# Another order of the steps in the first part of an attention and two-MoE kernel

## The chip, the cores and the metric

The kernel runs on one core of one Trainium2 chip. The metric is the device time of one execution in microseconds (us), taken as the median of several runs; lower is better. Engines are named as in the profile: PE is TensorE (PEld its weight loads), DVE is VectorE, ACT is ScalarE, POOL is GpSimd, SP is SyncE, which here only issues DMAs. Each engine works through its own queue in order.

## What is computed

Attention inside chunks of 64 positions (8 batches, 8 heads, 576 positions, head size 64), then two feed-forward blocks over the 4608 tokens. Cut to what matters:

```python
scores = 1/sqrt(D) * matmul(q_c, k_c^T)              # per chunk of 64
attn = exp(scores - max(scores)); attn /= sum(attn) + 1e-9
x = matmul(attn, v_c)                                # 4608 tokens x 512
h = maximum(maximum(x @ w1, x @ w2), x @ w3)         # d_ff 768
x = h @ w_out                                        # 512
h = maximum(x @ w_in, 0)                             # d_ff 2048
out = h * h @ w_out2                                 # 4608 x 512
```

## The kernel before

The tokens are cut into 36 attention tiles of 128 and into 9 blocks `b` of 512 tokens, four tiles each. The kernel has three parts in a row: attention with the first feed-forward block (`p` and `y` matmuls, L382), the second block's first product (`z`, L477) and its second (`o`, L528). All products work on numbers that are split into a high and a low half, so a product is three matmuls (high by high, high by low, low by high). Weights come as 64-bit numbers and are converted on the chip.

The change touches the first part's list alone: the string `order` (from L648), which writes out the order of the work for blocks 0 and 1 by hand. The loop at L669 goes through its tokens and issues each step's instructions; `tc.manual_schedule()` (L604) keeps that order in every engine's queue. So a token's place sets the place of its instructions on PE, DVE, ACT, POOL and SP at once, each only among the instructions of the same engine.

The tokens, with the engine that each step uses:

- Tiles 0 to 7 (`tile_steps`, L609). `qk5` and `v5` issue the loads of tile 5 (SP; 0.52 MB for q and k, 0.26 MB for v). `S5` scores (PE); `M5` maximum and difference (DVE, L299 and L302); `X5` exponential (ACT, L305); `N5` sum, plus 1e-9, reciprocal (DVE, L311 to L316); `G5` multiplication (POOL, L319); `T5` turning (PE, L325); `E5` copy of it (ACT, L334); `V5` the product with v, whose tile is named `X` (PE, L353); `H5` and `L5` high half (ACT, L363) and low half (DVE, L368).
- Weight units 0 to 23 (`unit`, L122). `U5` issues the load (SP, L133, 0.52 MB). `A5` takes the number apart (two ACT passes, L95 and L96); `C5` is three DVE instructions (L103, L105, L108); `s5` an addition (POOL, L150); `h5` high half (ACT, L153); `l5` low half (DVE, L156). Units 0, 1, 2 are the slices `w0_0`, `w1_0`, `w2_0` of the three first weights, 3, 4, 5 the slices `_1`, 6 and 7 the slices `wo0` and `wo1` of the output weight, and then four at a time: `w0_f`, `w1_f`, `w2_f`, `wof`.
- Products (`item_steps`, L637). `p` followed by b, f, w multiplies block b by slice f of weight w: 24 matmuls on PE into one of two PSUM buffers of tag "p" (`bufs` in L55). `q000`/`p000` and `q001`/`p001` are two halves of one product each; the `q` half needs tiles 0 and 1 alone. `ep` empties the buffer: for w = 0 a copy `s` on ACT (L410), for w = 1 the maximum `m` on DVE (L413), for w = 2 the maximum `h` on DVE (L417). `hh` and `hl`, followed by b and f, split that `h` (ACT L420, DVE L422). `y3` multiplies block 0's `h` of slice 3 by `wo3` (24 matmuls).
- `@` takes one step of the attention of tiles 8 and up, `~` the softmax work behind it.

Behind the tokens `S1` and `V1` four matmuls on zeros (`heat`, L593) are issued, and eleven ahead of the list. Raw weights go through a ring of four buffers (tag "in"), so a `U` waits for the `C` of an earlier unit.

Of the kernel before, what the change touches and what calls it, by code (L numbers as in the profile page):

```python
# [35 lines left out]
N0 = 2  # L36
# [6 lines left out]
def kernel(ctx: ExitStack, tc, qkv, w123, w_out, w_in2, w_out2, out):  # L43
# [228 lines left out]
    def att_load_v(t):  # L272
        if t >= NT1:
            return
        v = wp.tile([P, 2, 4, D], F32, tag="w", name="v")
        for j in range(2):
            r, o = slice(j * D, j * D + D), (j ^ t % 2) * D
            nc.sync.dma_start(v[o:o + D].rearrange("p c a d -> p (c a d)"), qkv[t, r, 1024:1536])
        v_t[t] = v
# [149 lines left out]
    def g2(b, f):  # L429
        if f == 0:  # L430
            yacc[b] = [ps_tile("acc", f"y{d}") for d in range(KD)]
        hp = h_t.pop((b, f))
        wh, wl = WO[f]
        for d in range(KD):
            a, c = d // 2, slice(d % 2 * P, d % 2 * P + P)
            mm_k(yacc[b][d], (wh[:, a, c], wl[:, a, c]), hp, f, f == 0, f == NF1 - 1)
        if f == NF1 - 1:
            for d in range(KD):
                ys = tmp("ys")
                if d % 2:  # L440
                    nc.vector.tensor_copy(ys, yacc[b][d])
                else:
                    nc.scalar.copy(ys, yacc[b][d])
                nc.sync.dma_start(y_d[b][:, d, :], ys)
            del yacc[b]
# [37 lines left out]
    def take(tag, name):  # L483
        t = tmp(name)
        nc.scalar.copy(t, bank[tag])  # L485
        return t
# [66 lines left out]
    def soften():  # L553

        for g in todo.pop(0) if todo else ():
            run(g)
# [36 lines left out]
    def heat(n):  # L593

        for i in range(n):
            nc.tensor.matmul(warm, lhsT=zero[:, 0:P], rhs=zero, start=True, stop=True)

    def go(*gens):

        for g in gens:  # L600
            next(g, None)
# [35 lines left out]
    def item_steps(b, f, w):  # L637

        for p in proj(W123[f, w], x_t[b], f"p{w}", 2 if (b, f, w) in split_items else 1):
            yield  # L640
        yield from p1_end(b, f, w, p)
# [4 lines left out]


    order = """  # L648
        qk0 qk1 v0 v1 U0 qk2 S0 v2 M0 S1 qk3 X0 v3 M1 N0 X1 U1 N1 A0 G0 U2 G1 T0 C0 S2 E0 qk4 s0
        h0 V0 M2 v4 T1 H0 l0 S3 E1 L0 X2 U3 V1 M3 H1 N2 qk5 X3 A1 L1 G2 v5 N3 q000 A2 C1 G3 qk6 T2  # L650
        S4 E2 v6 C2 s1 h1 V2 M4 qk7 h2 s2 T3 H2 v7 U4 U5 U6 E3 L2 X4 V3 l1 A3 N4 S5 H3 l2 G4 q001
        L3 M5 p000 C3 U7 X5 T4 ep000 S6 E4 N5 s3 h3 V4 M6 G5 S7 H4 l3 X6 T5 L4 p001 E5 N6 A4 M7 V5
        G6 A5 T6 ep001 p002 C4 U8 H5 E6 X7 L5 s4 h4 N7 A6 V6 ep002 G7 A7 p010 l4 C5 U9 H6 hh00 L6
        s5 h5 T7 C6 U10 ep010 p011 E7 A8 l5 s6 hl00 h6 C7 U11 V7 A9 p012 ep011 s7 l6 H7 C8 U12 h7
        A10 y0 L7 s8 h8 ep012 l7 hh01 l8 A11 hl01 p100 C9 U13 C10 U14 s9 h9 A12 p101 l9 s10 ep100
        C11 U15 h10 p102 ep101 h11 s11 l10 A13 C12 U16 p110 ep102 s12 h12 C13 U17 A14 hh10 l12 s13
        h13 p111 l11 ep110 A15 C14 U18 A16 l13 s14 p112 ep111 h14 C15 U19 A17 l14 s15 h15 y1 ep112
        C16 U20 hh11 A18 hl11 s16 h16 p020 C17 U21 A19 l16 s17 l15 h17 p120 C18 U22 ep020 A20 l17
        s18 C19 U23 h18 p021 ep120 A21 l18 s19 C20 h19 p121 ep021 h20 s20 C21 A22 p022 l20 s21 h21
        ep121 A23 l19 l21 C22 p122 ep022 h22 s22 C23 hh02 p030 ep122 h23 s23 hl02 hh12 l22 l23  # L660
        p130 ep030 hl12 hl10 p031 ep130 p131 ep031 y2 ep131 p032 p132 ep032 hh03 hl03 p040 ep132
        hh13 hl13 p140 ep040 p041 ep140 p141 ep041 y3 ep141 p042 p142 ep042 hh04 hl04 p050 ep142
        hh14 hl14 @ p150 ep050 ~ p051 ep150 ~ p151 ep051 @ y4 ep151 p052 @ p152 ep052 hh05 hl05 ~
        y5 ep152 hh15 hl15 ~
    """.split()

    att = steps(8, NT1)
# [1 line left out]
    for token in order:  # L669
        if token == "@":  # L670
            att.pop(0)()
            continue
        if token == "~":
            soften()
            continue
        kind, n = token.rstrip("0123456789"), token.lstrip(ascii_letters)
        if kind == "v":
            att_load_v(int(n))
        elif kind in ("qk", *"SMXNGTEVHL"):
            go(tiles[int(n)])  # L680
        elif kind == "U":
            U[int(n)] = units[int(n)]()
        elif kind in (*"ACshl",):
            U[int(n)][kind]()
        elif kind == "y":
            g2(0, int(n))
        else:
            b, f, w = map(int, (n + "2")[:3])
            if kind == "q" or kind == "p" and (b, f, w) not in items:
                items[b, f, w] = item_steps(b, f, w)  # L690
            go(items[b, f, w])
        if token in ("S1", "V1"):
            heat(4)
        if token == "y3":
            for load in (att_load_v, att_load):
                for t in (8, 9):
                    load(t)
# [48 lines left out]
    for b in range(NB):  # L746
        for g in range(NG):
            bank["at"] = None
            z(b, g, 1, "at", True)
            a, s1 = bank["at"], take("at", "s1")  # L750
# [9 lines left out]
            s5 = take("acc", "s5")  # L760
            next(more, None)
            z(b, g, 6, "at", False)
            s2 = take("at", "s2")
# [84 lines left out]
```

## Time and profile before

| | |
|---|---|
| median of 3 runs | 1397.73 us (1396.68 to 1398.42) |
| the profiled execution | 1396.79 us, span 1395.0 us |
| PE busy | 1369.1 us, 98% |
| DVE busy | 914.6 us, 66% |
| ACT busy | 521.8 us, 37% |
| POOL busy | 195.1 us, 14% |
| granted TensorE clock, mean of the span | 0.998 |

The span is the profiled stretch; the time of the execution holds a little more around it. A busy share is a mean over the three parts, which have different limits, so it has to be read by stretches of time. Matmuls overlap: the next one starts while the last one runs out, so a pause of PE looks a little shorter in busy time than it is.

### The profile page before, as it was taken

The page shows a single profiled execution, that of the slowest core. Times are in us where ns is not written, and L with a number is a line of the kernel's source. Part 1 is how long each engine was busy: PE and PEld are TensorE (multiplying, and loading weights), DVE is VectorE, ACT ScalarE, POOL GpSimd, SP SyncE. Part 2 cuts the span into 40 slices and gives each one's busy share as a digit, 9 for nine tenths or more (in the row PEclk, how much of TensorE's full clock was granted, in tenths as well). Part 3 has the DMA queues.
Part 4 walks back from the last instruction along what each step waited for, and adds up shares of the span by engine and source line. Part 5 has one row for each costly group of instructions (what it writes and reads, how often), then busy time and mean ns, then how long its engine had stood idle before and what let it go on. Part 6 is the DMA issues. An engine that isn't in the chain of part 4 may idle for free.

```text
span 1395.0 us, 32661 instructions
## 1 busy us (share of the span) xinstructions
PE 1369.1 (98%) x13699; PEld 1354.3 (97%) x13699; DVE 914.6 (66%) x1437; ACT 521.8 (37%) x904; POOL 195.1 (14%) x180
## 2 busy tenths in 40 slices
PE   7979999999999999999999999999999999999998
PEld 5879999999999999999999999999999999999998
DVE  7994456566666565723266666667677788877774
ACT  4661234333343343311233333333334444444442
POOL 2440023322423232300000000000000000000000
PEclk9999999999999999999999999999999999999999
DMA  9451244554645554716543333343598443434341
GB/s 270 140 170 43 87 132 148 186 190 140 228 145 181 184 173 131 263 47 228 181 164 124 140 142 143 138 144 136 192 347 300 145 144 123 137 135 152 122 139 43
DMA packets 101235, 222.33 MB, mean 159 GB/s; under 512 B 11232, under 2 KB 20448, under 8 KB 101088
## 3 DMA queue, kind: packets, MB, share of 16 engines
q1 hardware_dynamic: 101088, 220.25, 46.9%
q8 instruction: 107, 1.75, 0.5%
q14 instruction: 40, 0.33, 0.1%
HBM read 134.22 MB, written 85.98 MB: 158 GB/s over the span
## 4 chain that ended last, share of the span: by engine, by line
PE 86%; DVE 1%; issue 0%; POOLq 0%; POOL 0%; ACT 0%; DVEq 0%; ACTq 0%
PE o L528 25%; PE z L477 25%; PE p L382 25%; PE y L382 9%; PE X L353 1%; PE S L292 1%; PE T L325 1%; DVE pl L219 0%; DVE u L500 0%; POOL u L500 0%; POOLq L844 0%; DVE mx L299 0%; DVE sm L311 0%; DVE e L302 0%; DVE h L417 0%
## 5 line engine op out<-in xcount | busy, mean ns | idle before, releaser
L477 PE MATMUL z<-yxh,wih 128*128 128x256 f32 x560 | 154.9, 277 | 0.0
L477 PE MATMUL z<-yxh,wil 128*128 128x256 f32 x560 | 154.7, 276 | 0.0
L477 PE MATMUL z<-yxl,wih 128*128 128x256 f32 x560 | 154.7, 276 | 0.0
L528 PE MATMUL o<-wo2h,gl 128*128 128x256 f32 x504 | 140.7, 279 | 0.0
L528 PE MATMUL o<-wo2h,gh 128*128 128x256 f32 x504 | 140.4, 279 | 0.0
L528 PE MATMUL o<-wo2l,gh 128*128 128x256 f32 x504 | 140.2, 278 | 0.0
L528 PE MATMUL o<-wo2h,gxl 128*128 128x256 f32 x504 | 140.1, 278 | 0.0
L528 PE MATMUL o<-wo2h,gxh 128*128 128x256 f32 x504 | 139.9, 278 | 0.0
L528 PE MATMUL o<-wo2l,gxh 128*128 128x256 f32 x504 | 139.9, 278 | 0.0
L500 DVE TENSOR_TENSOR c<-z,s 128x512 f32<-128x512 f32 x108 | 74.4, 689 | 89.4 <-PE z L477 84.9
L420 ACT CAST hh<-h 128x512 fp32r<-128x512 f32 x54 | 33.6, 621 | 261.7 <-DVE h L417 242.5
L477 PE MATMUL z<-yh,wih 128*128 128x256 f32 x448 | 124.2, 277 | 0.0
L477 PE MATMUL z<-yh,wil 128*128 128x256 f32 x448 | 124.1, 277 | 0.0
L477 PE MATMUL z<-yl,wih 128*128 128x256 f32 x448 | 124.1, 277 | 0.0
L417 DVE TENSOR_TENSOR h<-p,m 128x512 f32<-128x512 f32 x54 | 37.1, 688 | 132.0 <-PE p L382 131.1
L500 POOL TENSOR_TENSOR u<-u,s 128x512 f32<-128x512 f32 x9 | 11.7, 1295 | 761.5 <-DVE u L500 761.5
L485 ACT COPY s<-z 128x512 f32<-128x512 f32 x108 | 63.3, 586 | 133.7 <-PE z L477 132.4
L477 PEld LDWEIGHTS z<-yxh,wih 128*128 128x128 f32 x560 | 105.2, 188 | 0.2 <-DVE c L500 0.2
L477 PEld LDWEIGHTS z<-yxh,wil 128*128 128x128 f32 x560 | 105.1, 188 | 0.0
L477 PEld LDWEIGHTS z<-yxl,wih 128*128 128x128 f32 x560 | 105.1, 188 | 0.0
L528 PEld LDWEIGHTS o<-wo2l,gh 128*128 128x128 f32 x504 | 94.9, 188 | 0.0
L528 PEld LDWEIGHTS o<-wo2h,gl 128*128 128x128 f32 x504 | 94.7, 188 | 0.0
(184 smaller groups left out, 4079.4 us busy)
## 6 DMA issues: line engine op xcount, KB each, us to landing
gd<-g SPq DMA_DIRECT2D x144, 256.0 KB, 2.0
gr<-gd SPq DMA_DIRECT2D x72, 512.0 KB, 4.0
qk<-in_qkv SPq DMA_DIRECT2D x28, 512.0 KB, 3.9
raw<-in_w_out SPq DMA_DIRECT2D x22, 512.0 KB, 3.7
v<-in_qkv SPq DMA_DIRECT2D x72, 128.0 KB, 5.7
raw<-in_w SPq DMA_DIRECT2D x18, 512.0 KB, 3.6
yd<-ys SPq DMA_DIRECT2D x36, 256.0 KB, 2.9
yr<-yd SPq DMA_DIRECT2D x18, 512.0 KB, 5.2
```

What stands on the lines that cost most here:

```text
L292: nc.tensor.matmul(s_t[t][o:o + D, h ^ t % 2, :], lhsT=q[r, h, :], rhs=k[r, h, :], start=True, stop=True,)
L325: nc.tensor.transpose(tp[:, p * P:(p + 1) * P], e[:, 2 * p:2 * p + 2, :].rearrange("p h k -> p (h k)"), ident)
L353: nc.tensor.matmul(xps_t[t][j * D:j * D + D, p, c * D:c * D + D], lhsT=v[o:o + D, c, p, :], rhs=et[o:o + D, p, q:q + D], start=True, stop= ...
L382: nc.tensor.matmul(dst[:, c], lhsT=lhs, rhs=rhs[:, c], start=first and i == 0 and j == 0, stop=last and j == len(pairs) - 1, skip_group_ch ...
L417: nc.vector.tensor_tensor(out=h, in0=p, in1=st[b], op=ALU.max)
L420: nc.scalar.copy(hh, h)
L477: nc.tensor.matmul(dst[:, a * HC:a * HC + HC], lhsT=l[:, a, w], rhs=r[:, k, :], start=first and a + k + j == 0, stop=j == 2, skip_group_ch ...
L485: nc.scalar.copy(t, bank[tag])
L500: (eng or nc.vector).tensor_tensor(out=t, in0=x, in1=y, op=ALU.add)
L528: nc.tensor.matmul(bank[i][:, m * HC:m * HC + HC], lhsT=l[:, a, t], rhs=r[:, a, :], start=g + m + a + j == 0, stop=g == NG - 1 and j == 2, ...
```

## The change

The string is replaced by another one. It holds the same tokens, each once, in another order, and every step issues the same instructions. Besides, the first loads of tiles 8 and 9 are issued behind the token `p041` where they were issued behind `y3`. The diff, cut to the beginning, the middle and the end of the list:

```diff
     order = """
-        qk0 qk1 v0 v1 U0 qk2 S0 v2 M0 S1 qk3 X0 v3 M1 N0 X1 U1 N1 A0 G0 U2 G1 T0 C0 S2 E0 qk4 s0
-        h0 V0 M2 v4 T1 H0 l0 S3 E1 L0 X2 U3 V1 M3 H1 N2 qk5 X3 A1 L1 G2 v5 N3 q000 A2 C1 G3 qk6 T2
...
-        C16 U20 hh11 A18 hl11 s16 h16 p020 C17 U21 A19 l16 s17 l15 h17 p120 C18 U22 ep020 A20 l17
-        s18 C19 U23 h18 p021 ep120 A21 l18 s19 C20 h19 p121 ep021 h20 s20 C21 A22 p022 l20 s21 h21
-        ep121 A23 l19 l21 C22 p122 ep022 h22 s22 C23 hh02 p030 ep122 h23 s23 hl02 hh12 l22 l23
...
-        y5 ep152 hh15 hl15 ~
+        U1 qk0 U2 U0 qk1 qk3 qk2 qk4 qk5 v0 v1 qk7 qk6 v2 v3 A1 C1 S0 s1 U5 v4 U3 M0 v5 A2 h1 C2 A0 l1
+        X0 C0 S1 M1 s0 U4 v7 U6 S3 N0 X1 S2 N1 G0 M3 G1 T0 S4 M2 X3 E0 S5 N3 X2 h0 T1 N2 V0 E1 G3 M4 V1
+        G2 T3 M5 X4 S7 s2 H1 H0 T2 N4 S6 E2 L0 h2 G4 X5 L1 V2 E3 l0 T4 M7 H2 V3 E4 q000 N5 H3 A5 L3 G5
+        V4 L2 C5 q001 H4 A3 T5 M6 s5 U9 v6 p000 C3 X6 A4 p001 N6 U7 ep000 X7 G6 E5 N7 T6 G7 ep001 V5 E6
+        l2 h5 T7 L4 s3 H5 V6 h3 p002 l3 H6 C4 E7 h4 s4 U8 p010 ep002 A6 l4 A7 L5 L6 p011 C7 A8 l5 ep010
+        U11 C6 V7 p012 H7 ep011 s6 U10 h6 L7 h7 s7 A9 p100 l6 ep012 C8 p101 C9 h8 U12 ep100 hh01 s9 A10
...
+        hl05 ~ y5 hh14 hh15 hl15 hl14 hl13 ~
     """.split()
...
-        if token == "y3":
+        if token == "p041":
```

How this moves the queues is shown at two places. The first is the beginning of SP's queue, which sets when data lands; `raw` is a weight unit, `q` and `k` are a tile's. Before:

```order
L265 DMA q_111<-in_qkv 128x512
L265 DMA k_112<-in_qkv 128x512
L265 DMA q_115<-in_qkv 128x512
L265 DMA k_116<-in_qkv 128x512
L278 DMA v_119<-in_qkv 64x512 x2
L278 DMA v_122<-in_qkv 64x512 x2
L133 DMA raw_127<-in_w123 128x1024
L265 DMA q_129<-in_qkv 128x512
```

Now:

```order
L133 DMA raw_113<-in_w123 128x1024
L265 DMA q_115<-in_qkv 128x512
L265 DMA k_116<-in_qkv 128x512
L133 DMA raw_121<-in_w123 128x1024
L133 DMA raw_125<-in_w123 128x1024
L265 DMA q_127<-in_qkv 128x512
L265 DMA k_128<-in_qkv 128x512
L265 DMA q_131<-in_qkv 128x512
```

Unit 1 has gone ahead of tile 0's q and k, units 2 and 0 ahead of tile 1's; the loads of v follow behind six tiles' q and k.

The second is DVE's queue at the steps that empty the PSUM buffers of the products of slice 2, with block 0's `m` and `h` of `p021` and `p022`. Before, from `l21` to the `h` of `p122`:

```order
L156 TENSOR_TENSOR w_5l<-r,w_5h 128x2x256
L103 TENSOR_SCALAR a<-a 128x512
L105 TENSOR_SCALAR a<-a 128x512
L108 SCALAR_TENSOR_TENSOR a<-raw,a 128x512
L417 TENSOR_TENSOR h<-p_1423,m_1412 128x512
L103 TENSOR_SCALAR a<-a 128x512
L105 TENSOR_SCALAR a<-a 128x512
L108 SCALAR_TENSOR_TENSOR a<-raw,a 128x512
L417 TENSOR_TENSOR h<-p_1462,m_1451 128x512
```

Now, from the `m` of `p021` on:

```order
L413 TENSOR_TENSOR m_1267<-p_1202,s_1157 128x512
L103 TENSOR_SCALAR a<-a 128x512
L105 TENSOR_SCALAR a<-a 128x512
L108 SCALAR_TENSOR_TENSOR a<-raw,a 128x512
L417 TENSOR_TENSOR h<-p_1240,m_1267 128x512
L156 TENSOR_TENSOR wo2l<-r,wo2h 128x512
L103 TENSOR_SCALAR a<-a 128x512
```

Before, the `h` of `p022` stands behind `C22`, the last conversion but one; now it stands behind `C15`, with nine conversions still to come.

## Rows read from the trace of the kernel before

**Rows 1.** The page, part 1: busy us (share of the span) and instructions.

```profile
PE 1369.1 (98%) x13699; PEld 1354.3 (97%) x13699; DVE 914.6 (66%) x1437; ACT 521.8 (37%) x904; POOL 195.1 (14%) x180
```

**Rows 2.** Windows: stretch, length, busy us of PE, PEld, DVE, ACT, POOL; clock, DMA.

```profile
0.00:25.00 25.00, 18.25 (x279) 13.28 (x281) 16.32 (x31) 10.65 (x18) 6.16 (x11) 0.93 0.95 266
25.00:50.00 25.00, 21.32 (x363) 20.18 (x359) 24.24 (x44) 17.27 (x32) 10.71 (x9) 1.00 0.63 180
50.00:75.00 25.00, 22.24 (x205) 21.19 (x205) 24.48 (x36) 14.51 (x26) 9.70 (x8) 1.00 0.49 153
75.00:100.00 25.00, 19.50 (x160) 18.69 (x158) 24.48 (x35) 14.95 (x27) 10.50 (x7) 1.00 0.52 167
100.00:125.00 25.00, 23.11 (x194) 22.68 (x195) 15.77 (x24) 6.95 (x12) 5.37 (x4) 1.00 0.35 101
125.00:1395.00 1270.00, 1264.71 (x12512) 1258.25 (x12510) 809.31 (x1272) 457.48 (x793) 152.71 (x142) 1.00 0.46 158
```

**Rows 3.** Waits of PE, 0 to 200 us: total, times, longest.

```profile
PE p L382 <- DVE m L413: 4.4, 3, 2.8
PE T L325 <- POOL e L319: 4.0, 4, 2.8
PE p L382 <- ACT s L410: 3.2, 3, 2.1
```

**Rows 4.** Timeline around p030: start, duration, engine, line, operation, [idle before <- releaser].

```profile
105.63 0.41 DVE L103 TENSOR_SCALAR a<-a 128x512 f32<-128x512 f32 x1
...
107.15 0.68 DVE L417 TENSOR_TENSOR h<-p,m 128x512 f32<-128x512 f32 x1
...
107.40 1.28 POOL L150 TENSOR_TENSOR r<-a,r 128x512 uint32<-128x512 uint32 x1 [2.85 <-DVE a L108]
107.75 1.22 DVE L103 TENSOR_SCALAR a<-a 128x512 f32<-128x512 f32 x1
...
107.89 0.50 PE L382 MATMUL p<-xh,w_3h 128*128 128x256 f32 x2 [0.83 <-DVE h L417]
```

**Rows 5.** Timeline of the first 32 us: loads' waiters and the durations of single steps.

```profile
5.03 1.15 PE L292 MATMUL S<-k,q 64*64 64x64 f32 x32
...
7.43 1.15 PE L292 MATMUL S<-k,q 64*64 64x64 f32 x32 [1.25 <-DMA k<-in_qkv]
...
10.95 0.67 ACT L95 ACTIVATE a<-raw 128x512 f32<-128x512 f32 x1 [0.25 <-DMA raw<-in_w]
...
12.31 0.66 PE L325 MATMUL T<-ident,e 128*128 128x128 f32 x4 [2.77 <-POOL e L319]
...
13.41 1.33 PE L292 MATMUL S<-k,q 64*64 64x64 f32 x32 [0.45 <-DMA k<-in_qkv]
...
14.47 1.98 PE L353 MATMUL X<-et,v 64*64 64x64 f32 x32
...
18.49 1.10 PE L353 MATMUL X<-et,v 64*64 64x64 f32 x32
...
18.71 0.69 DVE L299 TENSOR_REDUCE mx<-S 128x8 f32<-128x512 f32 x1 [0.91 <-PE S L292]
...
20.04 0.68 DVE L311 TENSOR_REDUCE sm<-e 128x8 f32<-128x512 f32 x1
...
21.08 0.64 DVE L368 TENSOR_TENSOR xl<-X,xh 128x512 fp32r<-128x512 f32 x1
...
21.30 1.05 POOL L319 TENSOR_TENSOR e<-e,rs 128x512 f32<-128x512 f32 x1 [5.16 <-DVE rs L316]
...
31.47 0.68 DVE L368 TENSOR_TENSOR xl<-X,xh 128x512 fp32r<-128x512 f32 x1
```

**Rows 6.** The chain that ended last: two of its pieces behind the list.

```profile
612.35 8.28 PE p L382 x72
...
623.35 8.28 PE p L382 x72
```

**Rows 7.** DMA in the first 40 us.

```profile
DMA packets 4741, 10.56 MB, mean 264 GB/s; under 512 B 640, under 2 KB 640, under 8 KB 4736
```

More of the change, by code (lines that the diff above doesn't have):

```diff
@@ L648 @@
     order = """
-        qk0 qk1 v0 v1 U0 qk2 S0 v2 M0 S1 qk3 X0 v3 M1 N0 X1 U1 N1 A0 G0 U2 G1 T0 C0 S2 E0 qk4 s0
-        h0 V0 M2 v4 T1 H0 l0 S3 E1 L0 X2 U3 V1 M3 H1 N2 qk5 X3 A1 L1 G2 v5 N3 q000 A2 C1 G3 qk6 T2
-        S4 E2 v6 C2 s1 h1 V2 M4 qk7 h2 s2 T3 H2 v7 U4 U5 U6 E3 L2 X4 V3 l1 A3 N4 S5 H3 l2 G4 q001
-        L3 M5 p000 C3 U7 X5 T4 ep000 S6 E4 N5 s3 h3 V4 M6 G5 S7 H4 l3 X6 T5 L4 p001 E5 N6 A4 M7 V5
-        G6 A5 T6 ep001 p002 C4 U8 H5 E6 X7 L5 s4 h4 N7 A6 V6 ep002 G7 A7 p010 l4 C5 U9 H6 hh00 L6
@@ L654 @@
[L654 to L657, printed above, removed]
-        C16 U20 hh11 A18 hl11 s16 h16 p020 C17 U21 A19 l16 s17 l15 h17 p120 C18 U22 ep020 A20 l17
-        s18 C19 U23 h18 p021 ep120 A21 l18 s19 C20 h19 p121 ep021 h20 s20 C21 A22 p022 l20 s21 h21
@@ L660 @@
-        ep121 A23 l19 l21 C22 p122 ep022 h22 s22 C23 hh02 p030 ep122 h23 s23 hl02 hh12 l22 l23
-        p130 ep030 hl12 hl10 p031 ep130 p131 ep031 y2 ep131 p032 p132 ep032 hh03 hl03 p040 ep132
-        hh13 hl13 p140 ep040 p041 ep140 p141 ep041 y3 ep141 p042 p142 ep042 hh04 hl04 p050 ep142
-        hh14 hl14 @ p150 ep050 ~ p051 ep150 ~ p151 ep051 @ y4 ep151 p052 @ p152 ep052 hh05 hl05 ~
-        y5 ep152 hh15 hl15 ~
+        U1 qk0 U2 U0 qk1 qk3 qk2 qk4 qk5 v0 v1 qk7 qk6 v2 v3 A1 C1 S0 s1 U5 v4 U3 M0 v5 A2 h1 C2 A0 l1
@@ new lines @@
+        p102 hl01 h9 ep101 s8 hh00 l9 A11 p110 ep102 l7 C10 A12 p111 ep110 l8 U14 C12 p020 s10 ep111 h12
+        C11 p112 hl00 h11 U15 U13 s12 ep020 h10 s11 p120 ep112 l10 A14 A15 C14 p021 ep120 s14 U18 h14
+        A13 l14 p022 hh11 l12 ep021 C15 p030 ep022 s15 U19 U16 hh02 h15 l11 C13 y0 h13 s13 U17 ep030
+        p121 l13 A16 hl02 C16 p031 ep121 h16 s16 A17 p122 ep031 hh10 hl11 A18 A19 y1 C19 l15 p130 ep122
+        C18 C17 h18 p032 ep130 s18 h17 U21 U22 U20 U23 p131 s17 s19 y2 ep131 l18 ep032 l17 p132 l16 A21
@@ L665 @@
+        hh03 C21 p140 ep132 h21 s21 h19 l21 p141 ep140 A20 p142 ep141 p040 ep142 C20 hl10 h20 p041 s20
+        hh13 ep040 l20 A23 hl03 p042 A22 ep041 y3 ep042 l19 C23 p050 @ h23 hh04 hl04 C22 p150 ep050 ~
+        s22 s23 p051 ep150 ~ h22 hh12 l22 hl12 p151 @ l23 ep051 p152 ep151 p052 @ y4 ep052 ep152 hh05
+        hl05 ~ y5 hh14 hh15 hl15 hl14 hl13 ~
     """.split()
```

## The prediction

> **What bounds the kernel now.** I read the page first, then the time cut into windows, then TensorE's waits, then the timeline at the largest waits. TensorE (PE) is busy for 1369.1 of 1395.0 us [rows 1], so all its idle time together is 25.9 us. The windows say where it lies [rows 2]: 6.75, 3.68, 2.76, 5.50 and 1.89 us in the first five stretches of 25 us, 20.6 us in all; in the 1270 us behind them only 5.3 us are left. A list that orders the first part can therefore give back at most some 20 us, 1.5% of the time, and whatever it gives back stays, because the rest is work of PE without gaps: an item that starts earlier ends earlier.
>
> The same windows show the limit of that first part: from 25 to 100 us VectorE (DVE) is busy for 24.2 to 24.5 of each 25 us, PE for 19.5 to 22.2. PE waits for DVE's `m`, for GpSimd's (POOL's) `e` and for ScalarE's (ACT's) copy `s` [rows 3]. `m`, `h` and `s` are what empties a PSUM buffer of tag "p". There are two, so a product can start only when the product two before it has been emptied.
>
> The last such wait shows it whole [rows 4]. DVE goes through the three instructions of `C22` from 105.63, then `h` at 107.15 (this is `ep022`), and p030, the first product on `w_3h`, starts on PE at 107.89, right after `h`. The `h` had stood behind conversions of weights. POOL's instruction from 107.40 then stretches DVE's next one to 1.22 us (the same L103 took 0.41 at 105.63), while `h`, which reads PSUM, kept its 0.68.
>
> **The measure.** I call "delay" of an item the time at which PE starts it, less PE's work that the list puts ahead of it. Prices: a scores step S and an output step V (its tile is `X`) 1.1 us, a turn T 0.55, a little under their durations in [rows 5], since the next step begins while one runs out; a product or a `y` step of 24 matmuls 2.75, as 96 take 11.00 us where nothing is waited for [rows 6]. Ahead of p030 stood 8 tiles (22.0 us) and 20 items (55.0): its delay is 107.89 - 77.0 = 30.9 us. Behind it PE runs on without a gap worth the name [rows 2], so 30.9 us is what the old list costs.
>
> DVE's work by its starts: C 1.52 (105.63 to 107.15), one tensor_tensor 0.60 (107.15 to 107.75) [rows 4]; M 1.33, N 1.04 [rows 5]. A POOL instruction costs DVE something too: from 31.47 [rows 5] to `ep022` at 107.15 DVE has 20 C, 3 M, 3 N and 37 tensor_tensor, 59.9 us, but took 75.7; 22 POOL instructions fall there, 0.72 us each. So old `ep022` ends after 23 C, 8 M, 8 N, 44 tensor_tensor (80.5) and 30 x 0.72, 102.1 us of DVE work; it ended at 107.83, an offset of 5.7. Delay = 102.1 - 77.0 + 5.7 = 30.8, which closes the sum.
>
> **The change, part by part.** No instruction comes or goes; busy sums stay.
>
> *Products.* In the old list whole conversions stand ahead of each release, in the new one they stand behind it where they can. DVE's work ahead of a release, less PE's ahead of the product that needs it, is 16.6 for p110, 16.7 for p020, 23.2 for p022, 25.1 for p030. By the same count the new list has its largest value at p100 (`L7`: 8 C, 8 M, 8 N, 17 tensor_tensor and 15 POOL, 52.2, less 38.5, 13.7), and then 12.4 at p110, 9.5 at p030, 3.4 at p130. The offset comes from the start, walked through next.
>
> *Loads.* Three weight units (0.52 MB each) go ahead of most q and k. S0 started at 5.03 behind 0.52 MB, S1 at 7.43 behind 1.05, S2 at 13.41 behind 2.62, the last two waiting for the transfer [rows 5]: 0.26 MB per us, and the mean of the first 40 us is 264 GB/s [rows 7]. New: unit 1 by 5.0, k0 (1.05 MB) 7.4, k1 (2.62) 13.4, k5 (4.72) 21.4, k6 (6.29) 27.3, v3 (6.82) 29.3, unit 5 31.3. So M1 ends some 7 us later than in the old list; `C1`, `C2`, `C0` fill part of it.
>
> *The clock.* The granted clock of the first 25 us is 0.93 [rows 2]: X at 14.47 took 1.98 us, at 18.49 1.10 [rows 5], half speed (1.2 of 2.4 GHz), after PE had stood idle for 2.77 us before 12.31. The new list leaves PE emptier still between 5 and 15 us, so I put S0, S1 and the four warming matmuls at half speed, which makes M1 0.9 us later (2.0 for 1.1). The Trainium skill (TensorE: Matmul & The Clock Gate, Part 1) says that an idle array falls back to 1.2 GHz, which speaks against this change; the row agrees, and where by that rule PE stayed at 1.2 GHz through its later waits the sum would be that of the second rival.
>
> *DVE's start.* S0 7.4 to 9.4, M0 10.8, C2 12.3, l1 12.9, C0 14.4. S1 13.4 to 15.4, M1 16.8, N0 and N1 18.9, M3 and M2 21.6, N3 and N2 23.7, one POOL hold 24.4, M4 and M5 27.1, N4 28.1, L0, L1, l0 29.9.
>
> *PE's start.* S5 (k5) 21.4 to 22.5, T1, V0, V1 25.3, four warming matmuls 26.3 (1.04 us), T3, S7, T2, S6, V2, T4, V3 32.7; all data has landed by then. q000 starts at 32.7: 16.0 us of work ahead, delay 16.7. That is later than in the old list, but S4 to S7, T2 to T4, V2 and V3 now stand ahead of it.
>
> *To the first full product.* V3's copy H3 on ACT 33.3 (an ACT pass is at most 0.67 [rows 5]), L3, L2 34.5, C5, M6, C3 38.9, N6 39.9; N7 waits for the exponential of tile 7, which stands behind A3, A4 and `ep000` on ACT, until 40.4, and ends 41.9 with a POOL hold; POOL's `e` 43.0 (1.05 [rows 5]); T7, V6, then p002 at 44.8. Work ahead 26.4, delay 18.4. DVE's `l2` ends about 43.6, counted 40.1 (5 C, 8 M, 8 N, 8 tensor_tensor, 12 POOL), an offset of 3.5; at p100 that makes 13.7 + 3.5 = 17.2, below 18.4. From here PE is the later of the two, and each release waits for its product, not for conversions.
>
> *Cover.* PE now hides the conversions. Between p002 and p132 stand 25 items; in the walk some eight releases come within 1.3 us of their need. If none slips, nothing is added; if each slips by one POOL hold, 8 x 0.72 = 5.8. Most margins are nearer 1 than 0, so I take 2.0. Behind the list nothing is late: DVE was busy for 15.8 us in 100:125 [rows 2] and has its last `l` long before p052.
>
> **Sum.** 30.9 - 18.4 - 2.0 = 10.5 us saved. The profiled execution took 1396.79 us (span 1395.0 and 1.8 around it): 1386.3. It lies 0.94 below the median of 1397.73, so I forecast **1387.2 us**. With the hold at 0 and the start 1 to 2 us better or worse its own range is 1384 to 1393.
>
> **Rivals.** *POOL holds DVE in full* (8%). For: L103 at 107.75. Against: the mean of 0.72 over 22. Place: the dense G and s steps before `L7`. At 1.28 us, the whole instruction [rows 4], 15 of them add 8.4 us: delay 13.7 + 8.4 + 3.5 = 25.6, with the 2.0 a gain of 3.3, 1394.4. This is the rule of the Trainium skill (SBUF — State Buffer, section "SBUF: two separate sides"): the pair of ports that both engines share is locked for a whole instruction. The trace agrees on what is held (L103, not `h`), not on the mean price.
>
> *The clock stays low* (6%; slower). If PE keeps 1.2 GHz not to about 17 but up to p002, the 5.1 us from T3 to V3 and the 10.4 from q000 to p002 take twice as long and lie on the path: p002 at about 60, delay 18.4 + 15.5 = 33.9, with the 2.0 5.0 us worse than before, 1402.7. It becomes slower from about 13 us of added PE time on. Against: once PE was busy from 14.47 the old run was back at 1.10 by 18.49.
>
> *The gain is handed on* (7%; no change). ACT's copies `s` stand among the A and h steps that DVE needs, and DVE's releases behind C; if each of the 25 items waits 0.42 us more, 10.5 us are gone, 1397.7. For: waits for `s` of 3.2 us in 3 cases [rows 3]. Against: the walk's margins. If the list on the chip did nothing, the time would be this as well.
>
> *Better* (7%). No slip, and a start 2 us sooner (TensorE at full clock, transfers faster): 30.9 - 17.2 + 1 is 14.7 saved, 1383.0.
>
> **How the numbers follow.** My forecast has 72%. A difference under 0.2% (2.8 us) can't be told from none. Faster: 0.72 + 0.08 + 0.07 = 0.87; same 0.07; slower 0.06. The range 1384.0 to 1394.5 holds the forecast's cases and the first rival; the low clock, the lost gain and most of the better case, some 18%, are left out.
>
> **What would show it.** Right: q000 near 33 and p002 near 45 us; PE's idle time in the first 125 us about 11 instead of 20.6, nearly all of it before 45; DVE below 24 of 25 us between 50 and 100, waiting for PE's `p`; p030 near 85 to 87 instead of 107.9; everything behind 130 us as before, some 10 us earlier. Wrong: PE waits for `m`, `h` or `s` after 50 us of over 4 us in sum (slips or holds), a clock below 0.85 in the first 25 us or below 1.00 in the second (clock), or p002 later than 50.

## The result, and the profile after

The changed kernel took 1383.15 us (median of 4 executions, 1382.38 to 1384.69), the kernel before in the same job 1397.34 us; the ratio is 0.9899, 95% interval 0.9887 to 0.9912. It is faster, by 14.2 us, where 10.5 were forecast. The time lies 0.85 us below the lower end of the range. In a second job (the run `again`, below) the same kernel took 1384.68 us (1383.38 to 1385.24) against 1397.11, 12.4 us less, and that lies inside the range: its own start differs from execution to execution, which the sections below take apart.

The page of the changed kernel, part 1, in the columns of [rows 1]:

```profile
PE 1368.1 (99%) x13699; PEld 1353.8 (98%) x13699; DVE 902.7 (65%) x1437; ACT 520.6 (38%) x904; POOL 194.8 (14%) x180
```

The span fell from 1395.0 to 1382.9 us and PE's work nearly stayed (1369.1 and 1368.1), so what went is PE's idle time. DVE's busy time fell by 11.9 us with the same 1437 instructions; the last section comes back to that.

The windows, in the columns of [rows 2]:

```profile
0.00:25.00 25.00, 16.69 (x281) 11.55 (x282) 18.32 (x36) 10.29 (x17) 8.63 (x13) 0.93 0.95 300
25.00:50.00 25.00, 23.97 (x343) 21.44 (x342) 19.10 (x38) 16.73 (x31) 8.45 (x7) 0.94 0.60 165
50.00:75.00 25.00, 25.00 (x241) 24.80 (x240) 21.89 (x35) 11.77 (x22) 8.51 (x6) 1.00 0.42 126
75.00:100.00 25.00, 25.00 (x220) 25.00 (x219) 16.78 (x30) 14.51 (x26) 6.78 (x5) 1.00 0.33 107
100.00:125.00 25.00, 25.00 (x221) 25.00 (x220) 12.04 (x21) 6.44 (x11) 5.15 (x4) 1.00 0.33 107
```

From 50 to 125 us PE has no gap at all, where [rows 2] show 2.76, 5.50 and 1.89 us idle in three stretches. DVE, which had been busy for 24.5 of 25, is down to 21.9 and 16.8. All that is left of PE's idle time in these 125 us lies in the first two stretches, 8.31 and 1.03 us. The waits of PE over the first 200 us, in the columns of [rows 3], name them:

```profile
PE S L292 <- DMA k<-in_qkv: 4.6, 2, 3.9
PE X L353 <- issue: 2.4, 1, 2.4
PE T L325 <- POOL e L319: 1.5, 2, 1.0
PE warm L596 <- DVE zero L77: 1.2, 1, 1.2
```

No wait for `m`, `s` or `h` is left. At p030, the place of [rows 4], the order of events has turned round; the timeline there, in the same columns:

```profile
84.86 1.29 POOL L150 TENSOR_TENSOR r<-a,r 128x512 uint32<-128x512 uint32 x1 [3.62 <-DVE a L108]
...
84.94 0.39 PE L382 MATMUL p<-xh,w_3h 128*128 128x256 f32 x2
...
85.14 0.69 DVE L417 TENSOR_TENSOR h<-p,m 128x512 f32<-128x512 f32 x1 [0.45 <-PE p L382]
```

PE starts p030 at 84.94 with no wait, and now it is the `h` (of p022) that waits 0.45 us for PE. 84.94 less 66.0 us of work ahead is a delay of 18.9 us, against 30.9: 12.0 less, and the two profiled executions differ by 1396.79 - 1384.69 = 12.1. The measure of the prediction holds.

The start of PE's queue in the changed kernel, in the columns of [rows 5]:

```profile
5.87 1.15 PE L292 MATMUL S<-k,q 64*64 64x64 f32 x32 [0.66 <-DMA k<-in_qkv]
10.94 1.93 PE L292 MATMUL S<-k,q 64*64 64x64 f32 x32 [3.92 <-DMA k<-in_qkv]
12.80 1.84 PE L596 MATMUL warm<-zero 128*128 128x512 bf16 x4
...
19.85 1.15 PE L353 MATMUL X<-et,v 64*64 64x64 f32 x32
23.42 1.15 PE L353 MATMUL X<-et,v 64*64 64x64 f32 x32 [2.42 <-issue]
24.50 1.74 PE L596 MATMUL warm<-zero 128*128 128x512 bf16 x4
26.03 1.06 PE L325 MATMUL T<-ident,e 128*128 128x128 f32 x4
...
41.64 0.66 PE L325 MATMUL T<-ident,e 128*128 128x128 f32 x4 [1.03 <-POOL e L319]
...
44.97 0.50 PE L382 MATMUL p<-xh,w_0h 128*128 128x256 f32 x2
```

S1 started at 10.94, not at 13.4, and ran at half speed (1.93), as did the four warming matmuls behind it. Then V1 (the second `X` row) waited for 2.42 us, and behind that pause the clock fell a second time: the second group of warming matmuls took 1.74 us, T3 1.06. The windows give the granted clock of both stretches:

```profile
11.00:14.50 3.50, 3.50 (x36) 2.11 (x36) 3.09 (x7) 0.69 (x3) 1.26 (x1) 0.51 1.06 390
24.70:28.10 3.40, 3.40 (x28) 2.28 (x28) 2.76 (x6) 0.98 (x2) 1.04 (x1) 0.50 1.05 256
```

p002 came at 44.97, behind 26.4 us of work (delay 18.6), and from there to p030 (delay 18.9) only 0.4 us were added (18.57 to 18.94).

### The profile page after: what moved, and what is told of

Its sections match the earlier page's. It is cut to its first block, busy times and chain, and to the rows that moved or that the text cites. A ratio compares the mean times of both kernels' runs of the same rounds, so it can differ in the third digit from the quotient of the medians.

```text
span 1382.9 us, 32659 instructions
## 1 busy us (share of the span) xinstructions
PE 1368.1 (99%) x13699; PEld 1353.8 (98%) x13699; DVE 902.7 (65%) x1437; ACT 520.6 (38%) x904; POOL 194.8 (14%) x180
## 4 chain that ended last, share of the span: by engine, by line
PE 86%; DVE 1%; issue 0%; POOLq 0%; POOL 0%; ACT 0%; ACTq 0%; DVEq 0%
PE o L528 25%; PE z L477 25%; PE p L382 25%; PE y L382 9%; PE X L353 1%; PE S L292 1%; PE T L325 1%; DVE pl L219 0%; DVE u L500 0%; POOL u L500 0%; POOLq L843 0%; DVE mx L299 0%; DVE sm L311 0%; DVE e L302 0%; DVE h L417 0%
```

## The experiments

Each kernel was timed against the kernel before on the same chip. The delay given is that of p030 in the profiled execution, less 77.0 us of work ahead in the order that the old list has there, 66.0 in the new one.

**Which part of the list brings the gain.** The new list up to p012 with the rest in the old order (`h_newfront`; its diff against the changed kernel is shown), and the reverse (`h_oldfront`).

```diff
         ep010 U11 C6 V7 p012
-        H7 ep011 s6 U10 h6 L7 h7 s7 A9 p100 l6 ep012 C8 p101 C9
+        hh00 U10 s6 hl00 h6 A9 ep011 s7 l6 H7 C8 U12 h7 A10 y0
...
```

> The new list up to p012, then the rest of the tokens in the old list's order. Theory (the gain lies in where DVE's releases of the two PSUM buffers stand among the conversions): the count of DVE's work ahead of the release less PE's ahead of the product is 24.9 us at p030 and 25.0 at p130, with the new front's offset of 3.5 a delay of 28 to 29 us at p030 instead of 18.8, so 9 to 10 us slower than the changed kernel, 1392 to 1394, and PE waits for m, h and s between 60 and 110 us. Rival (the gain lies in the front: loads, tiles, first products): 1383 to 1385, with no such waits.

> The old list up to p012, then the rest in the new list's order. Theory (releases): the largest lag is 14.2 us at p100, with the old front's offset of 5.7 a delay of about 20 us, so 1 to 2 us slower than the changed kernel, 1384 to 1386. Rival (the front): most of the gain is gone, 1393 to 1397.

`h_newfront` took 1395.65 us (ratio 0.9989, 0.9981 to 0.9998), `h_oldfront` 1384.15 us (0.9905, 0.9892 to 0.9919). The windows of 50:75 and 75:100 of `h_newfront`, then two of its waits of PE:

```profile
50.00:75.00 25.00, 22.80 (x211) 21.73 (x209) 23.93 (x36) 15.01 (x28) 10.54 (x8) 1.00 0.49 149
75.00:100.00 25.00, 19.57 (x159) 18.96 (x160) 24.45 (x35) 14.97 (x26) 11.27 (x8) 1.00 0.57 174
```

```profile
PE p L382 <- DVE m L413: 4.4, 3, 2.8
...
PE p L382 <- ACT s L410: 3.0, 3, 1.9
```

and the same windows of `h_oldfront`:

```profile
50.00:75.00 25.00, 25.00 (x237) 24.47 (x236) 23.71 (x35) 12.35 (x23) 9.93 (x7) 1.00 0.47 148
75.00:100.00 25.00, 25.00 (x220) 25.00 (x219) 16.16 (x29) 14.54 (x26) 6.46 (x5) 1.00 0.35 107
```

With the old order of the rest DVE is full again, PE has the gaps of [rows 2] back, and p030's delay is 28.5, as the count expected, although p002 stood at 42.56 (delay 16.2), earlier than in the changed kernel; the time is above the 1392 to 1394 us expected. With the new order of the rest the gaps are gone, whichever of the two fronts stands ahead. So the gain lies in the rest of the list, and the new front alone is worth 1.6 us. That it is the place of the releases among the conversions rests on the waits for `m`, `s` and `h`, which come and go with that part, and on the count. The new rest also has the products themselves in another order (`y0` and `y1` come later), and the two were not tried apart.

**Releases a little later.** The list is the one of `heat_none` (below). Its new place for `ep022` also makes that maximum take the copy of p030 instead of its own; the work is the same in kind and amount.

```diff
-        p100 l6 ep012 C8 p101 C9 h8 U12 ep100 hh01 s9 A10 p102 hl01 h9 ep101 s8 hh00 l9 A11 p110
+        p100 l6 C8 ep012 p101 C9 h8 U12 ep100 hh01 s9 A10 p102 hl01 h9 s8 hh00 l9 A11 ep101 p110
...
```

> The new list without the second group of warming matmuls (its time alone 1381.74), and with each release of VectorE from p100 to p132 put as late as the list allows, directly ahead of the product that needs its buffer, so that one or two conversions or subtractions more stand ahead of most releases. Theory (a count: VectorE's work ahead of a release less TensorE's work ahead of the product, plus VectorE's offset): the largest value rises from 13.7 at p100 to 14.3 at p101, with the offset of 0.7 to 1.0 that the trace shows there 15.0 to 15.3, still at or below TensorE's own delay of 15.6 to 15.7: 0 to 0.5 us, 1381.5 to 1382.4. Rival (each release is on the path, and what is put ahead of it is paid each time): 14 releases by 1 to 2 us, 1395 to 1405.

It took 1382.12 us (1381.85 to 1383.08) against 1381.74. PE's waits between 50 and 130 us hold one for a release:

```profile
PE p L382 <- DVE m L413: 0.2, 1, 0.2
```

From p110 to p030 the delay rose by 0.6 us. By the two lists twelve releases of DVE have one conversion or subtraction or more ahead of them that they had not; together they cost 0.4 (medians of two jobs) to 0.6 us (this trace), and the rival (each one paid) is 13 us and more away.

**How much room DVE has at the tightest place.** The list of `heat_none` again, with fills of a tile that nobody reads any more ahead of `L7`:

```diff
+        if token == "L7":
+            for _ in range(24):
+                nc.vector.memset(zero, 0.0)
```

> The new list without the second group of warming matmuls (1381.74), with 24 extra fills of the zero tile on VectorE ahead of L7, some 0.27 us each, 6.5 us in all; nobody reads them. It measures the cushion of VectorE at the tightest place of my count, p100. Theory: L7 ended at 52.83 after an idle 0.52 us, p100 started at 54.25, so VectorE has 1.9 us to spare there; what is beyond goes into TensorE's delay once and stays: 4.6 us (3.8 to 5.0), 1385.5 to 1386.8, delay of p100 and of p030 near 20.2 instead of 15.6. Rival 1 (TensorE's lead absorbs it, VectorE has much more room): below 1.5 us. Rival 2 (the releases behind it slip as well, each by a hold or so): 8 us and more, above 1389.5.

1390.69 us (1390.09 to 1394.12), 8.95 more than without the fills and not the 4.6 expected. The time is the one that rival 2 named (8 us and more), but its mechanism is not there: between 45 and 130 us PE waits once, at p100, and for no release behind it. The timeline shows the fills and `L7` on DVE, then PE at p100:

```profile
51.21 9.28 DVE L676 MEMSET zero<- 128x256 uint32 x24
60.41 0.63 DVE L368 TENSOR_TENSOR xl<-X,xh 128x512 fp32r<-128x512 f32 x1
61.09 0.58 PE L382 MATMUL p<-xl,w_0h 128*128 128x256 f32 x1 [6.76 <-DVE xl L368]
```

and the window behind it:

```profile
61.00:66.00 5.00, 4.91 (x23) 4.91 (x24) 4.14 (x9) 0.62 (x1) 0.55 (x1) 0.50 0.24 61
```

Two sizes were off. The fills took 9.28 us, 0.39 each, not 6.5. And PE's pause of 6.76 us dropped its clock to 0.50 for the next 5 us, which lost another 2.5. The cushion itself came out as counted: in `heat_none` `L7` starts 1.20 us behind the start of the `m` ahead of it (50.94 and 52.14), so here (`m` at 50.52) it would have started at 51.72; it was 8.7 us late and PE waited 6.8: 1.9 us of room.

**The warming matmuls.** Four kernels that change only the group of four matmuls on zeros behind V1; the output does not depend on them. `heat_v0` has the group behind V0, `heat_none` leaves the four out, `heat_one` leaves out three of them, `heat_p` writes them into a PSUM buffer of tag "p".

```diff
-        if token in ("S1", "V1"):
+        if token in ("S1", "V0"):     # heat_v0
+        if token in ("S1",):          # heat_none
             heat(4)
```

```diff
-            heat(4)
+            heat(4 if token == "S1" else 1)     # heat_one
```

```diff
+            if token == "V1":                   # heat_p
+                warm = ps_tile("p", "warm2")
             heat(4)
```

> The new list, with the second group of four warming matmuls behind V0 instead of V1, so that they fill PE's idle 2.4 us before V1 instead of standing between V1 and T3. Theory (in the profiled run a second spell at half clock behind that pause made the four, T3 and S7 1.6 us longer, and other runs lack it): the clock of 25 to 50 us is 1.00 in the profile, T3 starts near 24.7 instead of 26.0, and the time is 1381 to 1382.5 with a spread under 1 us. Rival (the start is set by the loads and DVE alone): within 0.5 us of the changed kernel.

> The new list without the second group of four warming matmuls. If the clock falls behind the pause before V1 as in the profiled run: T3 to V3 at half speed in part, the 1.7 us of the four saved and 1 to 3 us lost, 1382 to 1385. If the clock needs no such help here: 1381.5 to 1382.5, like the group behind V0.

`heat_v0` 1382.81 us (1382.52 to 1383.09), `heat_none` 1381.74 (1381.55 to 1381.81). `heat_v0` came out a little above its forecast and within the 0.5 us of its rival, though its trace has the clock of 1.00 in 25:50 and T3 at 24.96 as expected. `heat_none` came out as forecast, with a spread of 0.26 us where the changed kernel has 2.3, and all its executions are faster than any of the changed kernel; its ratio to the kernel before is 0.9888 (0.9875 to 0.9902). PE's timeline of `heat_none` at V0 and V1, which now run as one, and DVE's at M4's second instruction:

```profile
21.09 1.91 PE L353 MATMUL X<-et,v 64*64 64x64 f32 x64
```

```profile
23.16 0.69 DVE L302 TENSOR_TENSOR e<-S,mx 128x512 f32<-128x512 f32 x1
```

V1 no longer waits. That looked like a gain of the matmuls' own time, but one thing did not fit: with the group V1 had started, in every trace then at hand, 0.1 us behind the end of this L302. In the changed kernel it ended at 22.62 + 0.69, and V1 started at 23.42:

```profile
22.62 0.69 DVE L302 TENSOR_TENSOR e<-S,mx 128x512 f32<-128x512 f32 x1
```

The tile `warm` is one of the four PSUM buffers of tag "acc" and is held until its last matmul, so that V1 has to wait for the buffer of S4, which M4 empties. The two kernels that follow tell the buffer from the matmuls.

> The new list with one warming matmul behind V1 instead of four (three matmuls on zeros are left out, the output does not depend on them). What is to be told apart is what made the list without the second group 2 to 3 us faster. Theory: the tile of the warming matmuls holds one of the four PSUM buffers of tag acc until its last matmul; so V1 must wait for the buffer that M4 on VectorE empties (V1 starts 0.1 us behind the end of M4's second instruction in all four traces that have a later group, and right behind V0 without it). One matmul keeps the buffer as four do: V1 waits about 2 us for M4 again, and the time stays at 1382.7 to 1384.5. Rival: the gain came from the time of the four matmuls, 1.04 us, of which 0.78 is left out here: V1 right behind V0, 1381.7 to 1382.3.

> The new list with all four warming matmuls behind V1, but written into a buffer of tag p, so that the one of tag acc comes free after the first group. Theory (the buffer): V1 starts right behind V0, before M4 ends, the four matmuls fill time in which TensorE has little to do, and the time is 1381.6 to 1382.8. Rival (the matmuls' own time, or V1 waits for something else): V1 again 0.1 us behind M4, 1383.0 to 1385.0.

`heat_one` took 1383.54 us (1382.18 to 1384.61), `heat_p` 1381.70 (1381.52 to 1384.00). M4's second instruction and V1 in `heat_one`:

```profile
22.78 0.69 DVE L302 TENSOR_TENSOR e<-S,mx 128x512 f32<-128x512 f32 x1
...
23.57 1.94 PE L353 MATMUL X<-et,v 64*64 64x64 f32 x32 [1.90 <-issue]
```

and V0 with V1, then the group, in `heat_p`:

```profile
20.47 1.91 PE L353 MATMUL X<-et,v 64*64 64x64 f32 x64
22.54 0.81 PE L596 MATMUL warm<-zero 128*128 128x512 bf16 x3 [0.16 <-DMA k<-in_qkv]
```

One matmul brings the wait and the time of the changed kernel back; with four in another buffer V1 does not wait, and three of the four executions are as fast as those of `heat_none` (the fourth took 1384.00). It is the buffer that V1 waits for.

**The changed kernel again, and its second hunk undone.**

```diff
-        if token == "p041":
+        if token == "y3":      # y3back; the run again has no edit
```

> The changed kernel itself once more, in another job. Its four times lay at 1382.4, 1382.5, 1383.8 and 1384.7, and the profiled one (1384.69) showed the granted clock at half speed a second time, at 24.7 to 28.1 us. Theory: the second stretch at half speed comes in some executions only and costs about 2 us, so the times fall between 1382.3 and 1384.8 again, and if this profiled execution is one without it (clock 1.00 in 25:50), q000 starts near 30.6 and p002 near 42.6 us, as in the list that had the new front alone. Rival: the second stretch belongs to every execution and the times differ for another reason; then the clock in 25:50 is below 1.00 again in an execution near 1382.5.

> The new list with its second hunk undone: the first loads of tiles 8 and 9 are issued behind y3, as before, and not behind p041. Theory: no difference, within 1 us of the changed kernel (1382.4 to 1384.7), since TensorE shows no wait for data behind 45 us and the first step on tile 8 stands 10 tokens behind y3. Rival: the loads come late for the first step on tile 8, and TensorE waits for k there, 1 to 4 us (1384 to 1388).

`again` 1384.68 us (1383.38 to 1385.24), `y3back` 1384.47 (1382.87 to 1385.56): the second hunk makes no difference, and no wait for k or v stands behind 45 us in the trace of `y3back`. The profiled execution of `again` has the pause before V1 (1.89 us) and a clock of 0.96 in 25:50, and took 1384.52; that of `y3back` has the pause (2.16 us), a clock of 1.00 there, a delay 1.0 us smaller and took 1383.78. So the second stretch at half speed stands behind the pause, but not in every execution that has the pause. The mean clock of the span goes with the time of the eight executions of the changed kernel: 0.999 at 1382.4 and 1382.5, 0.996 to 0.998 at 1383.4 to 1385.2. In which stretch the six executions that were not profiled lost their clock isn't known.

In `y3back` q000 stood at 31.83 and not near 30.6. But its first stretch at half speed was a long one, from 9 to 17 us, as in `again`, where q000 stood at 32.86; in the changed kernel's first trace it lasted from 11 to 15 us. The trace to hold beside that one is `h_newfront`, whose list is the same up to p012. It has the pause, no second stretch (clock 1.00 in 25:50), and q000 2.42 us sooner:

```profile
22.60 1.15 PE L353 MATMUL X<-et,v 64*64 64x64 f32 x32 [2.42 <-issue]
...
30.42 0.38 PE L382 MATMUL p<-xh,w_0h 128*128 128x256 f32 x1
```

An estimate from these rows: with `h_newfront`'s delay of 16.2 at p002 and the 0.4 behind it, the changed kernel would take some 1365.8 + 16.6 = 1382.4 us, which is what its two fastest executions took.

**An earlier start.** Two lists on the base of `heat_none`, with k1 ahead of two weight units.

```diff
-        U1 qk0 U2 U0 qk1 qk3
+        U1 qk0 qk1 U2 U0 qk3                                    # both
-        M0 v5 A2 h1 C2 A0 l1 X0 C0 S1 M1 s0
+        M0 v5 X0 S1 M1 A2 h1 C2 A0 l1 C0 s0                     # front2
+        M0 v5 X0 S1 M1 X1 N0 A2 h1 N1 G0 C2 A0 l1 C0 s0         # best
...
-        p000 C3 X6 A4 p001 N6 U7 ep000 X7 G6
+        p000 X6 A4 p001 N6 C3 U7 X7 ep000 G6                    # best
```

> The new list without the second group of warming matmuls (1381.74), with q and k of tile 1 loaded ahead of units 2 and 0, and S1, M1 and the exponential of tile 1 put ahead of the conversions C2 and C0. Theory (TensorE's delay is set by the landing of k1 and the half clock that follows: S1 starts at 11.43 and TensorE runs without a gap of over 0.4 us from there to 37): k1 comes behind 1.57 instead of 2.62 MB, S1 starts at about 7.5 to 8, and what is gained is bounded by VectorE, which was idle for 1.24 us between 7.7 and 13.4: 0.5 to 1.3 us faster, 1380.4 to 1381.2. Rival (VectorE's work in a row from 5 us on sets the start, and its order makes no difference): 1381.5 to 1382.

> The new list without the second group of warming matmuls, with q and k of tile 1 loaded ahead of units 2 and 0, S1, M1, X1, N0 and N1 ahead of the conversions C2 and C0 (the list that moved S1 and M1 alone left T0 waiting 2.64 us for N0), S2 ahead of M3, and the exponential of tile 7 ahead of the copy ep000 on ScalarE, C3 behind N6. Theory: what is left of TensorE's delay is the landing of k1 (S1 at 11.43), the half clock behind it and the wait of T6 for N6 (1.24 us); with these moved p002 starts 1 to 1.5 us earlier than at 41.84, and the time is 1380.2 to 1381.0. Rival: VectorE's work in a row up to N7 sets p002 whatever the order in front, as the list with S1 and M1 moved suggested: 1381.4 to 1382.6.

`front2` 1382.56 us (1381.76 to 1383.45), `best` 1382.46 (1381.71 to 1383.09): no gain, if anything 0.7 worse. `best` lies within its rival's range, `front2` above both of its own. In `front2` S1 did start sooner, but the next wait is longer:

```profile
8.54 1.15 PE L292 MATMUL S<-k,q 64*64 64x64 f32 x32 [1.09 <-DMA k<-in_qkv]
...
17.64 0.89 PE L325 MATMUL T<-ident,e 128*128 128x128 f32 x4 [2.64 <-POOL e L319]
```

From 14 to 35 us DVE is busy for 19.8 to 20.0 of 21 us in all three lists (`heat_none` and these two), and a turn ahead of p002, T6 in `heat_none` and T7 in the others, waits for POOL's `e` behind DVE's `N6` or `N7`. That DVE's work in a row sets p002, whatever is loaded first, is read off these traces and is not the whole of it: p002 came 1.6 to 1.8 us later in the two (43.64 and 43.48, against 41.84), and in `front2` `N7` itself waits 1.79 us for ACT's exponential.

**All runs in one measure.** Profiled execution, p030's delay, and the difference, in us:

| kernel | time | delay | rest |
|---|---|---|---|
| before | 1396.79 | 30.9 | 1365.9 |
| h_newfront | 1394.70 | 28.5 | 1366.2 |
| pad_hn | 1390.69 | 24.9 | 1365.8 |
| h_oldfront | 1384.87 | 19.0 | 1365.9 |
| changed | 1384.69 | 18.9 | 1365.8 |
| again | 1384.52 | 18.9 | 1365.6 |
| heat_one | 1384.61 | 18.4 | 1366.2 |
| y3back | 1383.78 | 17.9 | 1365.9 |
| front2 | 1383.45 | 17.6 | 1365.8 |
| rel_late_hn | 1383.08 | 17.1 | 1366.0 |
| best | 1383.09 | 17.5 | 1365.6 |
| heat_v0 | 1382.52 | 17.0 | 1365.5 |
| heat_p | 1381.64 | 15.4 | 1366.2 |
| heat_none | 1381.55 | 15.8 | 1365.8 |

Over a range of 15 us the time is 1365.5 to 1366.2 plus the delay. Nothing that happens behind p030 takes part.

## Why the prediction was right, and where it failed

- **The bound and the measure: right.** The gain came off PE's gaps between 25 and 110 us, the gaps came from the rest of the list (`h_newfront`, `h_oldfront`), by their waits and the count from releases behind conversions, and a delay once gone stays gone (the table).
- **Products: right.** The count put the tightest place at p100, 17.2, and below PE's own delay. (With the prices as printed the 59.9 us of DVE's work is 59.7, the 80.5 is 80.3 and the price of a POOL instruction 0.73; the 102.1 stays.) In the changed kernel `L7` ended at 55.96, an offset of 3.8 over the counted 52.2, where 3.5 was put; no product behind p002 waited. The cushion at p100 is 1.9 us (`pad_hn`).
- **The start: the right number by two errors.** q000 at 32.84 (forecast 32.7) and p002 at 44.97 (44.8). But *Loads* failed: S0 started at 5.87, not at 7.4, and k1 had landed by 10.94, not at 13.4; the 0.26 MB per us came from stretches with other loads. The windows of 8 to 14 us, before and then in the changed kernel, have the rate in their last column:

```profile
8.00:14.00 6.00, 2.79 (x48) 1.78 (x45) 5.18 (x10) 2.74 (x5) 2.09 (x2) 1.00 1.04 273
```

```profile
8.00:14.00 6.00, 3.06 (x35) 2.21 (x36) 5.14 (x10) 3.39 (x6) 1.32 (x2) 0.75 1.05 395
```

  The lead, 2.5 us at S1 and some 3 at V0, was given back before V2 by two things that the walk did not have: V1's wait for a PSUM buffer (2.42 us), and behind it the second stretch at half speed, some 1.6 us in the rows above (1.74 for 1.04, 1.06 for 0.66, and S7's 1.63 for 1.15).
- **The clock: half right.** S1 and the first group ran at half speed as put, S0 did not (1.15 us). That the clock would fall again behind a later pause was left to a rival: behind V1's pause of 1.9 to 2.4 us it fell in the changed kernel, `again` and `heat_one`, and not in `y3back` and `h_newfront`. The rule of the Trainium skill (TensorE: Matmul & The Clock Gate, Part 1), that an idle array falls back to 1.2 GHz, names the level that the first three of these traces show; it doesn't tell them from the other two. The page says as well that the number of slow matmuls differs from run to run, and the traces agree: 0.94 and 0.96 in 25:50 in two executions, 1.00 in that of `y3back`.
- **Cover: the term that was mis-sized.** I put 2.0 us for releases that slip; from p002 to p030 it was 0.4. "Most margins are nearer 1 than 0" counted each margin by itself. But they are margins of one queue: by the prediction's own count the lag falls from 13.7 at p100 to 9.5 at p030 and 3.4 at p130, so DVE gains on PE with nearly each product, and what one release loses the next has back. Twelve releases made later cost 0.4 to 0.6 us (`rel_late_hn`). With 0.4 in its place the sum is 30.9 - 18.4 - 0.4 = 12.1, and the two profiled executions differ by 12.1.
- **From the profiled execution to the median: failed.** I added 0.94 us, since the profiled execution of before lay that far below its median. That of the changed kernel lay 1.54 above its own. It had the second stretch at half speed; that the faster executions lacked it fits their mean clock of 0.999 and the estimate from `h_newfront`, but no trace of them shows it. These 2.5 us and the 1.6 of *Cover* are the miss of 4.05. In the second job (median 1384.68 against 1384.52) only the latter would have been left.
- **Busy sums stay: wrong for DVE**, 11.9 us less. It did not move the time, because DVE no longer paces PE.
- **Rivals.** POOL holding DVE in full, a clock low up to p002 and a gain handed on did not come. The *better* case (no slip, a sooner start; 1383.0) is what three of the eight executions show (1382.4, 1382.5 and 1383.4), and 7% was too little for it: of its conditions no slip and faster transfers came in both traces of the changed kernel. The sooner start came in neither (p002's delay 18.6 in both); what the clock did in the three is not known.

## What to carry to other kernels

When two engines share in-order queues, count each one's cumulative work ahead of every hand-over and compare the largest difference with the start's delay. The count told p030's delay ahead to about 1 us where it was tried (28 to 29 for 28.5, about 20 for 19.0), the delay as measured carried the time of all fourteen profiled executions to within 0.7 us, and small reorderings below the largest difference cost next to nothing. A tile that is only written to keep an engine busy still occupies its buffer; look at what waits for the buffer before the filler's own time is blamed. And before a profiled execution stands for the median, see whether its start is one that every execution has.

## What the runs showed of the hardware that I had not expected

- A pause of PE costs twice when the clock falls behind it: in `pad_hn` a wait of 6.76 us was followed by 5 us at 0.50, some 9.3 us together.
- From 8 to 14 us the DMA moved 395 GB/s in the changed kernel, where q, k and weight units (128 rows each) were on their way and v's transfers were only being issued (from 11.49), and 273 in the kernel before, where v's transfers of 64 rows stood among them; in the changed kernel it fell to 262 in 16:19, when its v loads had begun. That v's shape is the cause was not tried by itself.
- DVE's instructions got shorter. The groups of the first 130 us, before and then changed (count, busy us, mean ns):

```profile
L103 DVE TENSOR_SCALAR a<-a 128x512 f32<-128x512 f32 x24 | 18.7, 777 | 0.0
```

```profile
L103 DVE TENSOR_SCALAR a<-a 128x512 f32<-128x512 f32 x22 | 11.2, 511 | 4.3 <-ACT a L95 4.3
```

  POOL's addition starts when a conversion ends. In the old list the next conversion's L103 often stood right there and was held, as in [rows 4]; in the new one it is often a release, which reads PSUM and kept its 0.69 us under POOL's instruction at 84.86. So the order also decides how much of POOL's time DVE pays: an effect of a few tenths of a microsecond for each conversion, which a price of 0.72 for every POOL instruction cannot show. That it is this and not another neighbour was read off the traces, not tested.
